# Attention and gated convolution on one core: a new order of all steps, q of batch 0 turned in row pairs, and 46 fillers in four places

## The chip, the cores and the metric

The kernel runs on one core of one Trainium2 chip. The metric is the device time of one execution in microseconds. Work goes to five engines, each with an instruction queue of its own that it works off in order: PE (TensorE, matrix products into the banks of PSUM), DVE (VectorE), ACT (ScalarE), POOL (GpSimd) and SP (SyncE, which only issues transfers here). PE's loading of a stationary operand is listed apart as PEld. Semaphores make an instruction wait for what other engines or transfers must have done.

## The reference

Eight batches, eight heads, 576 tokens, head size 64. First a linear attention without softmax, with a norm over each head, then a gated unit whose gate is a causal convolution over five tokens:

```
kv  = einsum('bhsd,bhse->bhde', k, v)                 # 64 x 64 per batch and head
out = einsum('bhsd,bhde->bhse', q, kv)
x   = out / sqrt(mean(out*out, -1) + 1e-6) * g_norm   # then (B, S, H*D) = (8, 576, 512)
gate_pre[s] = sum over k < 5 of conv_w[k] * x[s - 4 + k]
val = x @ w_val                                       # 512 x 512
result = (sigmoid(gate_pre) * val) @ w_out            # 512 x 512
```

Inputs q, k, v and g_norm are float32; the three weights are stored as float64, so the kernel makes float32 of them itself, in pieces.

## The kernel before

The program is a list of some 1,235 steps, `PLAN`, written out as text; the loop at the end of the kernel calls one small function for each, in that order. The order in the text is the order on each engine's queue; no scheduler changes it. What a step waits for follows from the tiles that it shares with earlier steps. Tiles come from pools with a number of rotating buffers: eight PSUM banks (`ps`), three output tiles `ot`, two `x`, and so on; the next request takes the next buffer in turn.

What the steps do, in the order in which a batch meets them:

- `load_q_rows`, `load_half`, `load_q`, `stage_weight` issue the transfers: q of batches 0 and 1 in two halves by heads, k and v in two halves each, q of later batches by head pairs, the weights in quarters (`wval` 0 to 3, `wout` 0 to 3, and `cw`, the taps of the convolution with g_norm).
- `narrow_weight key n` is one of eight pieces that turn a quarter from float64 into float32: pieces 0, 4, 5, 6 and 7 on DVE, 1, 2 and 3 on ACT. `turn_cw` (PE) and `keep_cw` (DVE) turn the taps.
- `start_warm` runs matmuls of the identity with itself, whose result nobody reads.
- `kv_product b i` (36 matmuls of 64x64, each two rows of the profile) and `kv_copy` (ACT).
- q of batches 0 and 1 is turned on PE by `turn_q_rows` (L477) and put in order by `sort_q` (L484); q of later batches is turned on DVE by `turn_q`.
- `raw_whole` (batch 0, L512), `raw_pair` and `raw_tail` (L501) multiply q by kv; `square`, `sums`, `powers` (POOL, L552) and `normalise` make the norm. Token blocks, called 0 to 3 with 128 tokens and 4 with 64, each have a step.
- `turn_x` (L583) and `keep_x`, or for later batches `turn_blocks` and `move_blocks` (a transfer within SBUF), bring x into columns; `halo` (POOL) copies the rim for the convolution.
- `gate_start`, four `gate_tap` (DVE, L621, 128 of them in all, each adding into the tile that the one before wrote), `gate_end` (the sigmoid, ACT) and `gated` (DVE, L646) make the gate.
- `val_product` (batches 0 and 1, L633) or `val_fast` (L682, seven products in place of eight, with sums of blocks from `x_sums` and `val_sums`) make the values.
- `token_sums` (DVE, L752), `fast_product` (L774), `fast_keep` (DVE or ACT) and `store` make the output of the 512 tokens of a batch pair's halves; `out_product` (L720) that of the last 64 tokens.

At the start of the program the first steps are

```
load_q_rows 0 1; stage_weight cw 0; load_q_rows 0 0; load_half v 0 0; load_half k 0 0; narrow_weight cw 0 5;
...
narrow_weight cw 0 2; warm_up; stage_weight wval 1; stage_weight wval 0; start_warm 36; turn_q_rows 0 3;
turn_q_rows 0 2; turn_q_rows 0 0; kv_product 0 0; turn_q_rows 0 1; sort_q 0 0; sort_q 0 1; narrow_weight cw 0 3;
narrow_weight cw 0 4; narrow_weight cw 0 7; turn_q_rows 0 4; turn_cw; keep_cw; kv_product 0 1; sort_q 0 4;
sort_q 0 3; kv_copy 0 0; kv_copy 0 1; narrow_weight wval 1 5; narrow_weight wval 1 0; sort_q 0 2; raw_whole 0 3;
```

and the functions that the change touches, with what calls them, are:

## Time and profile before

| | |
|---|---|
| time, median of 3 runs | 304.87 us (304.09 to 306.43) |
| span of the profiled execution, first to last instruction | 304.6 us |
| PE busy | 294.8 us, 97% of the span |
| weight loads (PEld) | 232.4 us, 76% |
| DVE busy | 269.2 us, 88% |
| ACT busy | 193.7 us, 64% |
| POOL busy | 114.9 us, 38% |
| moved by transfers | 55.53 MB, 182 GB/s on average |

The profiled execution has no time of its own beside its span. A matmul in float32 stands in the profile as two rows, a transpose as one. Matmuls overlap in PE, so a PE that is always busy may still be slowed: its rate is read from the starts of its rows. The granted clock is 1.00 when PE gets its full rate.

### The profile page before, as it was taken

What the parts mean: (1) busy time and instruction counts of PE and PEld (TensorE: products, weight loads), DVE (VectorE), ACT (ScalarE), POOL (GpSimd) and SP (SyncE); (2) the same over time, 40 slices, a digit from 0 to 9 for tenths busy, and PEclk for the clock granted to TensorE, in tenths of its full rate; (3) what the DMA queues carried; (4) which work ended last, traced back from release to release, by engine and by line L of the source; (5) the groups of instructions that cost most, each with busy time, mean ns of one, the idle gap of its engine ahead of it and who ended that gap; (6) DMA issues with size and microseconds to landing.
All of it is one profiled execution on the core that took longest, in us unless ns stands there. A gap on an engine that the chain in (4) does not pass through costs nothing.

```text
span 304.6 us, 8977 instructions
## 1 busy us (share of the span) xinstructions
PE 294.8 (97%) x3441; PEld 232.4 (76%) x3441; DVE 269.2 (88%) x474; ACT 193.7 (64%) x596; POOL 114.9 (38%) x127
## 2 busy tenths in 40 slices
PE   7899999999999999999999999999999999999993
PEld 7788778877787785777778757787878588888582
DVE  1169999999999999999999999999999999999612
ACT  1569989999768664884586547683787354535220
POOL 3027354406568217364338352345536631000000
PEclk9979999999999999999999999999999999999999
DMA  7999998088569756988689477927411621112423
GB/s 269 343 368 343 272 302 210 4 230 269 154 147 329 231 163 167 269 220 260 173 253 294 111 175 232 326 72 214 114 48 30 169 80 34 36 42 64 103 69 103
DMA packets 32074, 55.53 MB, mean 182 GB/s; under 512 B 6166, under 2 KB 14358, under 8 KB 32032
## 3 DMA queue, kind: packets, MB, share of 16 engines
q1 hardware_dynamic: 29520, 49.76, 55.7%
q0 software_dynamic: 1632, 3.17, 4.1%
q10 hardware_dynamic: 880, 2.03, 1.8%
q8 instruction: 27, 0.44, 0.6%
q14 instruction: 15, 0.12, 0.1%
HBM read 39.21 MB, written 9.44 MB: 160 GB/s over the span
## 4 chain that ended last, share of the span: by engine, by line
PE 89%; DVE 5%; DMA 2%; issue 1%; ACT 1%; DVEq 0%; ACTq 0%; SPq 0%
PE a L774 18%; PE cb L774 14%; PE va L682 13%; PE val L633 11%; PE vc L682 6%; PE kvps L440 6%; PE raw L501 5%; PE out L720 5%; PE vb L682 4%; PE qTps L477 4%; PE raw L512 2%; PE xTps L583 2%; DMA qs<-in_q_dram 2%; DVE gate L621 2%; DVE xs L667 1%
## 5 line engine op out<-in xcount | busy, mean ns | idle before, releaser
L552 POOL TENSOR_TENSOR rt<-ss,mhalf 128x8 f32<-128x8 f32 (+3 forms) x38 | 68.9, 1822 | 101.0 <-DVE ss L544 100.8
L621 DVE SCALAR_TENSOR_TENSOR gate<-xT,cwT,gate 128x576 f32<-128x576 f32 x128 | 101.8, 809 | 1.0
L571 ACT ACTIVATE x<-raw,rt 128x64 f32<-128x64 f32 x252 | 55.8, 351 | 7.2 <-POOL rt L552 4.2
L604 POOL DMA_DIRECT2D xT<-y x48 | 26.4, 557 | 25.5 <-DVE ot L784 14.0
L633 PE MATMUL val<-xT,wval 128*128 128x288 f32 x128 | 33.0, 411 | 0.0
L774 PE MATMUL a<-wsum,sums 128*128 128x256 f32 x128 | 32.4, 382 | 0.0
L628 ACT ACTIVATE gate<-gate 128x576 f32<-128x576 f32 x32 | 22.0, 692 | 11.7 <-DVE gate L621 11.4
L633 PEld LDWEIGHTS val<-xT,wval 128*128 128x128 f32 x128 | 23.5, 190 | 6.5 <-ACT xT L590 0.4
L544 DVE TENSOR_REDUCE ss<-sq 128x8 f32<-128x520 f32 (+1 forms) x40 | 24.7, 627 | 2.9 <-ACT sq L531 2.5
L774 PEld LDWEIGHTS a<-wsum,sums 128*128 128x128 f32 x128 | 24.0, 190 | 4.1 <-issue 0.6
L535 ACT ACTIVATE sq<-raw 128x256 f32<-128x256 f32 (+1 forms) x70 | 22.4, 403 | 7.3 <-PE raw L501 7.1
L682 PE MATMUL va<-xs,vsum 128*128 128x288 f32 x96 | 26.6, 409 | 0.0
L615 ACT ACTIVATE gate<-xT,cwT 128x576 f32<-128x576 f32 x32 | 25.2, 811 | 1.5 <-DVE gv L646 1.3
L646 DVE TENSOR_TENSOR gv<-gv,gate 128x576 f32<-128x576 f32 x32 | 23.6, 750 | 0.9 <-ACT gate L628 0.8
L682 PEld LDWEIGHTS va<-xs,vsum 128*128 128x128 f32 x96 | 18.0, 190 | 5.1 <-ACT x L571 0.4
L611 POOL COPY xT<-xT 128x124 f32<-128x124 f32 x32 | 17.5, 585 | 10.5 <-ACT xT L590 10.5
L501 PEld LDWEIGHTS raw<-kv,qT 64*64 64x64 f32 x1008 | 16.4, 134 | 5.3 <-issue 3.0
L440 PEld LDWEIGHTS kvps<-v,k 64*64 64x64 f32 x1008 | 15.9, 135 | 3.7 <-issue 1.9
L501 PE MATMUL raw<-kv,qT 64*64 64x64 f32 x1008 | 18.7, 221 | 0.0
L440 PE MATMUL kvps<-v,k 64*64 64x64 f32 x1008 | 17.6, 220 | 0.0
L774 PE MATMUL cb<-wsum,sums 128*128 128x256 f32 x64 | 16.9, 386 | 0.1
L774 PE MATMUL cb<-wout,gv 128*128 128x256 f32 x64 | 16.8, 385 | 0.0
(111 smaller groups left out, 542.3 us busy)
## 6 DMA issues: line engine op xcount, KB each, us to landing
qs<-in_q_dram SPq DMA_DIRECT2D x96, 140.0 KB, 4.2
out_dram<-ot SPq DMA_DIRECT2D x140, 64.0 KB, 1.7
k<-in_k_dram SPq DMA_DIRECT2D x14, 576.0 KB, 6.3
v<-in_v_dram SPq DMA_DIRECT2D x12, 576.0 KB, 6.5
xT<-y SPq DMA_DIRECT2D x48, 64.0 KB, 2.7
xT<-y POOLq DMA_DIRECT2D x48, 64.0 KB, 3.3
y<-in_moe_w_val_dram SPq DMA_DIRECT2D x4, 512.0 KB, 11.4
w_wout<-in_moe_w_out_dram SPq DMA_DIRECT2D x4, 512.0 KB, 6.3
```

Source lines behind the costliest of these rows:

```text
L440: nc.tensor.matmul(st["kvps", b][s][r * D:(r + 1) * D, i], st["k", b, i][rows, r, cols], st["v", b, i][rows, r, cols], start=(j == 0), sto ...
L501: nc.tensor.matmul(st["raw", b, c][r][cols, to * D:(to + 1) * D], st["qT", b][rows, hp, first:first + D], kvs[b % 2][rows, hp, :], start=T ...
L544: nc.vector.reduce_sum(out=st["ss", b][:, FIRST[c]:FIRST[c] + n], in_=st["sq", b, c][:, 0:n], axis=AX.X)
L552: nc.gpsimd.tensor_tensor(out=st["rt", b][:, which], in0=st["ss", b][:, which], in1=mhalf[:, which], op=ALU.pow)
L571: nc.scalar.activation(out=x[:, to * D:(to + 1) * D], in_=raw[:, h * D:(h + 1) * D], func=AF.Copy, scale=root[:, to:to + 1])
L604: (nc.sync if i % 2 else nc.gpsimd).dma_start(out=xTs[b % 2][i * TB:(i + 1) * TB, :, first:first + P], in_=y[a * TB:(a + 1) * TB, i])
L615: nc.scalar.activation(out=gate[:], in_=xTs[b % 2][:, jt, HALO:SX], func=AF.Copy, scale=cwT[:, K - 1, jt:jt + 1])
L621: nc.vector.scalar_tensor_tensor(out=gate[:], in0=xTs[b % 2][:, jt, tap * TB:tap * TB + S], scalar=cwT[:, tap, jt:jt + 1], in1=gate[:], op ...
L633: nc.tensor.matmul(val[:], wval[:, kc, jt * P:(jt + 1) * P], xTs[b % 2][:, kc, HALO + n * SV:HALO + (n + 1) * SV], start=(kc == 0), stop=( ...
L646: nc.vector.tensor_tensor(out=both, in0=both, in1=st["gate", b, jt][:], op=ALU.mult)
L682: nc.tensor.matmul(st[bank, "val", b, mj][:], weights_[:, k], tokens()[:, k], start=(n in (0, 1, 3) and k == 0), stop=(k == NK // 2 - 1), ...
L774: nc.tensor.matmul(st[bank, i, p], tokens()[:, k], weights_[:, k], start=(n < 2 and k == 0), stop=(k == NK // 2 - 1), skip_group_check=True)
```

## The change

Every step of `PLAN` stands at a new place, and the pools are gone: each tile that rotated is now one of a fixed set of rooms, and the step's text says which room it takes (`@` and a number; PSUM banks are rooms 0 to 7). q of batch 0 is turned as pairs of rows, 18 transposes of 128x128 in place of 36 matmuls of 64 columns, and sorted by 20 copies of 64 partitions, half on ACT and half on DVE, in place of five on ACT. `kv_copy` of batch 0 is split between ACT and DVE. `start_warm` takes a width: 36 matmuls of 38 columns at the start, and 3, 6 and 1 of 256 columns later, 46 in all. The table of the sigmoid is loaded first.

```diff
+    PAIRED_Q = (0,)
...
+    def new(tag, shape, dtype, name):
+
+        room = rooms[tag][picked.pop(0)]
...
     def ps(shape, name):
-        return psum.tile(shape, FP32, tag="bank", bufs=8, name=name)
+        return new("bank", shape, FP32, name)
...
-    def start_warm(n):
-
+    def start_warm(n, width):
+
+        reps = -(-width // P)
+        bank = ps([TB, reps, width // reps], f"warm{n}")
         for _ in range(n):
-            nc.tensor.matmul(warm_bank()[0:TB, 0, 0:TB], ident[:, 0:TB], ident[:, 0:TB], start=True, stop=True)
+            nc.tensor.matmul(
+                bank[0:TB], ident[:, 0:TB], ident[:, 0:width // reps].unsqueeze(1).broadcast_to((P, reps, width // reps)),
+                start=True, stop=True)
...
             for r in range(2):
                 rows = slice(r * D, (r + 1) * D)
-                nc.scalar.copy(
+                (nc.vector.tensor_copy if r else nc.scalar.copy)(
                     out=kv_bd[rows, :, rows].rearrange("p (i s) e -> p s i e", s=2)[:, s], in_=ps_[rows])
...
+        st["pq", b, j] = pq = ps([P, HB, P], f"qTps{b}_{j}")
+        if b in PAIRED_Q:
+            for r in range(2):
+                for n in range(0, m, 2):
+                    nc.tensor.transpose(
+                        pq[:, r * 2 + n // 2, :],
+                        qs[:, r, j * HB + n:j * HB + n + 2, :].rearrange("p n d -> p (n d)"), ident[:])
+            return
...
+        for r in range(2):
+            for e in range(2):
+                (nc.vector.tensor_copy if b == 0 and r else nc.scalar.copy)(
+                    out=qT[r * D:(r + 1) * D, j * HB + e:j * HB + m:2],
+                    in_=pq[e * D:(e + 1) * D, r * 2:r * 2 + m // 2])
```

The new list begins and ends with

```
load_q_rows 0 1; load_q_rows 0 0; load_half v 0 1 @ 0; load_half k 0 1 @ 0; start_warm 36 38 @ 0;
load_half v 0 0 @ 0; stage_weight wval 1; warm_up; load_half k 0 0 @ 0; stage_weight wval 0;
stage_weight cw 0 @ 0; turn_q_rows 0 4 @ 1; turn_q_rows 0 2 @ 0; turn_q_rows 0 1 @ 2; turn_q_rows 0 3 @ 3;
sort_q 0 1 @ 0; turn_q_rows 0 0 @ 4; start_warm 3 256 @ 5; sort_q 0 0; load_q_rows 1 0; stage_weight wval 3;
sort_q 0 3; load_q_rows 1 1; sort_q 0 2; kv_product 0 1 @ 2 4; stage_weight wval 2; load_half k 1 1;
narrow_weight cw 0 0 @ 0; start_warm 6 256 @ 3; narrow_weight cw 0 5 @ 0; load_half v 1 1;
narrow_weight cw 0 1; sort_q 0 4; narrow_weight cw 0 2; narrow_weight cw 0 3; narrow_weight wval 1 0 @ 1;
stage_weight wout 0 @ 1; narrow_weight cw 0 4; narrow_weight wval 1 1; narrow_weight cw 0 6 @ 1;
narrow_weight cw 0 7; narrow_weight wval 1 2; turn_cw @ 1; kv_product 0 0; keep_cw; load_half v 1 0;
narrow_weight wval 1 5 @ 1; narrow_weight wval 1 3; narrow_weight wval 1 6 @ 0; start_warm 1 256 @ 1;
kv_copy 0 1; kv_copy 0 0; load_half k 1 0; narrow_weight wval 0 0 @ 0; raw_whole 0 4 @ 3;
...
gate_end 7 2; gated 7 3; fast_product 3 1 6; gated 7 2; fast_product 3 1 5; fast_keep 3 1 6;
token_sums 3 1 0 @ 1; store 3 3; out_product 3 8 @ 2; fast_keep 3 1 5; token_sums 3 1 2 @ 2; token_sums 3 1 1;
store 3 2; token_sums 3 1 3; fast_product 3 2 1 @ 0; fast_product 3 2 3; fast_keep 3 2 1 @ 0; keep_out 3 8 @ 1;
...
```

In the instruction order of the two kernels the numbers differ only in what is named here: PE has 18 transposes more, 36 matmuls of q less and 10 wide fillers more; DVE has 12 copies more; ACT has two copies more and one table load less; SP and POOL have as many instructions as before. Of DVE's 128 taps, 27 stood directly behind a tap of the same gate, and 10 do now; of the sums of blocks (`x_sums`, `token_sums`) 10 stood directly behind the one that they read, and 3 do now.

## The prediction

> **What bounds the kernel now.** I read the engines' totals first, then busy time by stretch with the granted clock, then the matrix engine's timeline, then VectorE's timeline; last, the waits and the instruction order of the two kernels. The totals:

> ```profile
> PE 294.8 (97%) x3441; PEld 232.4 (76%) x3441; DVE 269.2 (88%) x474; ACT 193.7 (64%) x596; POOL 114.9 (38%) x127
> ```

> Two engines are near full. By stretch (columns: length, then busy us of PE, weight loads, DVE, ACT, POOL, then granted clock, DMA share, GB/s):

> ```profile
> 13.90:17.10 3.20, 1.53 (x73) 1.39 (x73) 2.29 (x8) 1.67 (x6) 0.00 (x0) 1.00 0.75 239
> 17.10:17.70 0.60, 0.55 (x2) 0.35 (x2) 0.60 (x3) 0.55 (x3) 0.00 (x0) 0.70 1.08 438
> 17.70:21.10 3.40, 3.40 (x20) 2.84 (x20) 1.80 (x4) 2.99 (x5) 0.17 (x1) 0.55 1.01 371
> ...
> 15.84:32.00 16.16, 15.60 (x254) 13.68 (x246) 13.37 (x26) 13.77 (x27) 8.75 (x5) 0.89 0.96 347
> 32.00:200.00 168.00, 167.36 (x2233) 129.31 (x2232) 166.54 (x284) 124.04 (x407) 75.81 (x83) 1.00 0.76 218
> 200.00:283.77 83.77, 83.52 (x646) 66.43 (x645) 81.00 (x132) 46.96 (x145) 27.95 (x32) 1.00 0.30 80
> ```

> Between 32 and 200 us both PE and VectorE run at 99%: there is nearly nothing idle to win there. What is lost lies in the first 30 us: PE works 1.53 of 3.20 us at 13.9 to 17.1, and the clock granted just after is 0.55. PE's timeline shows it:

> ```profile
> 1.36 4.05 PE L430 MATMUL warm<-ident 128*32 128x32 f32 x72 [1.36 <-POOL ident masks.py:199]
> 6.12 5.05 PE L477 MATMUL qTps<-ident,qs 128*64 128x128 f32 x48 [0.70 <-DMA qs<-in_q_dram]
> 15.05 0.21 PE L414 MATMUL cwps<-ident,cw 21*128 21x21 f32 x1 [1.22 <-issue]
> 17.15 6.32 PE L512 MATMUL raw<-kvbd,qT 128*128 128x128 f32 x40 [0.56 <-ACT kvbd L450]
> 23.40 2.84 PE L477 MATMUL qTps<-ident,qs 128*64 128x128 f32 x48
> 30.23 1.09 PE L583 MATMUL xTps<-ident,x 128*128 128x128 f32 x8
> ```

> The same 48 rows of q take 5.05 us at the start and 2.84 later: the start runs cold, though no throttle record marks it. The 40 rows of raw (128 columns each, 0.11 us warm as in xTps, half of that for the eight 64-wide ones, 3.8 to 4.0 in all) take 6.3: 2.3 us are lost to the clock.

> **PE's work from raw on.** At full rate, by the rows of the chain of waits (two fast products in 1.73 us, a fast val piece 0.97, four plain val products 7.96, a tail product 3.58): 112 fast products x 0.863 = 96.7; 84 val pieces x 0.97 = 81.5; 16 val products x 1.94 = 31.0; 4 tails 14.0; 14 kv products x 1.05 = 14.7; raw 15.5 + 4.0; q and x turns 9.4. That is 266.8. Each passage between wide matmuls and the 64x64 ones costs about 0.1 us; these edges sum to 9.3, so 276.1. Measured from 17.15 to the end of the last matmul at 299.3: 282.2. The rest, 6.1, is 2.3 of clock and 3.8 of true waits: 0.8 for the last token sums at 288.0, 0.4 before 282.5, some 0.4 before 31, 2.2 spread.

> **The change, part by part.**
> Row pairs: q of batch 0 takes 18 transposes instead of 36 matmuls. A 128-column transpose is 0.11 us warm (the eight rows of xTps from 30.23 to the first val at 31.16), so 2.0 us instead of 4.2; cold, twice that. In exchange sort_q grows from five copies to twenty of 64 partitions, ten on ACT (0.35 us by qT 128x256) and ten on DVE (0.42 by the copy at L797), DVE's each behind ACT's for the same part. DVE adds 4 us, before its dense stretch begins, where it idled 5.2 and 6.7 us.

> The walk to raw: q lands at 6.12 as before (the two q loads still lead their queues). With the clock full from 7.4 the ten transposes that sort_q 0 1 needs end near 8.0, all 18 at 8.7; three fillers (0.43 each) follow. ACT's four sorts end at 11.0, DVE's at 11.9. The pieces of cw are queued behind them: DVE's first at 12.0, ACT's three (0.40 each, with the last sort between) until 13.8, DVE's last three (0.28) until 14.8. turn_cw follows at 14.85 (15.05 before). kv product and copies: 15.0 to 16.2, then DVE's copy, queued behind keep_cw and two pieces of wval (1.6 us), ends at 17.2. Splitting kv_copy over two engines saves 0.5 and gives it back there. So raw starts at 17.25, against 17.15: I expect no gain. If all q work were warm from 6.1 and DVE did not queue, 16.1; if the clock stayed half until 14.2, 20.0. I take 17.25, since only the fillers' width (38 for 32, which closes 5.4 to 5.9) changes ahead of it.

> The ten fillers of 256: 4.3 us of PE, hidden in PE's idle time before cw and kv data. If that cover is gone (cold, twice the price) they push turn_cw itself. They fill the gap that preceded the half clock: 14.2 to 17.7 goes from 1.9 to about 2.2 busy us of 3.4, and the stretch before it from 3.0 to 3.2. Whether that suffices no row shows; the nearest kept stretch, 10.8 to 13.9, was 98% busy. Bounds: raw in 4.0 or 6.3. I take 4.0: gain 2.3.

> [...]

> After raw: turn_q_rows 1 0 is given the bank that normalise 0 3 still reads (0.2 us late by POOL's 2.06 us power), the turns of x wait for ACT 0.65 in all. Waits before the first val product 0.85 instead of 0.4.

> New order, DVE: an operation that uses the result just ahead of it starts later:

> ```profile
> 267.83 3.25 DVE L621 SCALAR_TENSOR_TENSOR gate<-xT,cwT,gate 128x576 f32<-128x576 f32 x4
> ...
> 169.22 0.79 DVE L621 SCALAR_TENSOR_TENSOR gate<-xT,cwT,gate 128x576 f32<-128x576 f32 x1
> 169.94 0.44 DVE L689 TENSOR_TENSOR gv<-vc,gv 128x288 f32<-128x288 f32 x1
> ```

> Four taps of one gate take 0.81 us each; a tap with a stranger behind it gives way after 0.72. In the order, taps directly behind a tap of the same gate fall from 27 to 10, dependent sums from 10 to 3: 24 x 0.1 = 2.4 us off DVE. That is no gain by itself: PE is as full. It is bounded by 0 and 2.9.

> DVE's own end: from the first piece of wval to the last gated 260.9 us busy (the three DVE numbers above), plus 2.0 for cw, keep_cw and kv copies now behind it, less 2.4, started at 13.6, with the 4.2 idle of before after 32 and 0.4 early: 278.7; with the 20.0 from there to the end, 298.7. So PE sets the end.

> New order, PE: 24 groups of 64x64 matmuls instead of 26 and 31 wide stretches instead of 35: edges 8.5, not 9.3. At the end the first token sum no longer stands behind a keep that waits for PE, and out_product 3 8 (3.6 us) covers it: the 0.8 at 288.0 goes, and I drop the 0.4 ahead of it. The other 2.2 I leave; 0 and 5 are its bounds. SP's loads of batch 1's q go out near 9 instead of 14 and 17, and DMA idle at 14 to 16 (152 GB/s) is used; nobody waits for it.

> **Sum.** 17.25 + 275.3 + 0.85 + 2.2 = 295.6 for the last matmul; 5.3 behind it as now (299.3 to 304.6): a span of 300.9. The page gives the profiled execution its span alone, 304.6; the median of the runs, 304.87, lies 0.27 above. So 301.2.

> **Rivals.**
> The fillers don't hold the clock: raw at half rate, 301.2 + 2.3 = 303.5. For it: 2.2 of 3.4 us is still far from the kept 98%. Against: no gap is as long as 1.2.

> Cold start, the other side. Transposes and 32-column fillers may not warm the clock: the 72 warm rows did not in 4 us, and no row here shows a transpose doing so. Then 18 transposes take 3.9, three fillers 2.6, kv 2.4, six fillers up to 5.2, in PE's order ahead of turn_cw. If the first full clock comes at 17.7, raw starts at 21.2 and the end is 305.2; with raw at half clock as well, 307.5. It is slower than before from a raw start near 21 on. Against it: the q matmuls alone warmed it by 10.8. [...]

> New waits in the middle: with PE and DVE both at 99%, one wrong order makes each wait for the other. 3 us more gives 304.2, 7 gives 308.2. For it: 32 to 200 was nearly free of waits, so there is more to lose than to win; rooms are now fixed by hand. Against: DVE gets 2.4 us of air.

> Better: the 2.2 of waits vanish and raw starts at 16.1: 297.9.

> **How the numbers follow.** Forecast 0.45 (own range 299.5 to 302.8), better 0.16, fillers fail 0.13, middle waits 0.16, cold start 0.10. A measurement here tells about 1% from nothing, so faster means below 301.8: seven tenths of the forecast, 0.32, all of better, and a little of the others make 0.50. Slower, above 307.9, is the far part of middle waits and of the cold start: 0.12. The rest, 0.38, is same. The range reaches from better to the cold start: 297.8 to 305.4.

> **What would show it.** Raw (40 rows) starting at 17 to 17.5 and taking 4 us at clock 1.00; cwps near 14.9; 18 transposes in 2 to 3 us from 6.1; the first val near 28.4; DVE busy for 2 us less at the same work; no wait of cb for sums near the end. I am wrong if the clock falls before 21 us, if raw starts after 20, or if PE's waits between 32 and 284 exceed 5 us.

## The result, and the profile after

The changed kernel takes 307.13 us (median of 8 runs, 305.69 to 308.16), the kernel before 304.75 (8 runs, 304.09 to 306.43). The ratio is 1.007, 95% interval 1.0044 to 1.0096: slower by 0.7%, where the prediction said 301.2 and at most 305.4.

One number first, since the sum rests on it. In every execution whose time and span are both known, the time is the span plus 1.74 to 1.90 us. After's profiled execution has a span of 306.4 and took 308.16, the slowest of its eight. Before's, with a span of 304.6, was therefore the run of 306.43, the slowest of its three, and not one near the median. Of 88 later executions of before, 57 have a mean granted clock of 0.995 or more and a median of 304.29 us, 31 a lower one (mostly 0.993) and a median of 306.05. The execution that the prediction was read from has 0.993.

After's totals, then busy time by stretch (length, PE, weight loads, DVE, ACT, POOL, granted clock, DMA share, GB/s):

```profile
PE 294.8 (96%) x3407; PEld 231.4 (76%) x3407; DVE 272.5 (89%) x486; ACT 194.1 (63%) x598; POOL 111.5 (36%) x127
```

```profile
13.90:17.10 3.20, 1.84 (x48) 1.08 (x47) 2.67 (x11) 2.60 (x5) 0.00 (x0) 1.00 1.06 375
17.10:17.70 0.60, 0.60 (x33) 0.54 (x33) 0.35 (x1) 0.00 (x0) 0.00 (x0) 1.00 1.15 395
17.70:21.10 3.40, 3.06 (x31) 2.40 (x27) 2.89 (x7) 2.38 (x6) 0.00 (x0) 1.00 1.07 379
15.84:32.00 16.16, 15.24 (x277) 13.05 (x274) 15.23 (x33) 12.71 (x24) 8.85 (x7) 1.00 1.05 387
32.00:200.00 168.00, 166.21 (x2237) 130.68 (x2236) 164.85 (x284) 122.80 (x400) 76.11 (x80) 1.00 0.73 205
200.00:285.64 85.64, 84.16 (x647) 66.32 (x646) 80.24 (x130) 48.50 (x152) 24.15 (x32) 1.00 0.36 92
```

The clock is 1.00 in every stretch, as the fillers were expected to make it. But between 32 and 200 us PE is busy for 166.2 us where it was for 167.4, and DVE for 164.9 where it was for 166.5: both wait more. PE's timeline of the head:

```profile
6.28 2.66 PE L513 MATMUL bank<-ident,qs 128*128 128x128 f32 x18
11.97 2.78 PE L463 MATMUL bank<-ident 128*32 128x256 f32 x12
15.52 0.21 PE L450 MATMUL bank<-ident,cw 21*128 21x21 f32 x1 [0.78 <-ACT wexp L404]
15.66 0.81 PE L475 MATMUL bank<-v,k 64*64 64x64 f32 x39
17.05 0.73 PE L475 MATMUL bank<-v,k 64*64 64x64 f32 x33 [0.58 <-issue]
18.66 4.43 PE L560 MATMUL bank<-kvbd,qT 128*64 128x128 f32 x40 [0.34 <-DVE kvbd L485]
29.86 2.21 PE L681 MATMUL bank<-xT,wval 128*128 128x288 f32 x8
```

The 18 transposes take 2.7 us and the 40 rows of raw 4.43, but raw starts at 18.66 instead of 17.25: the turn of cw is late, the kv product stops after 39 rows for 0.58 us with nothing to wait for, and the first product with wval comes at 29.86, not 28.4. In the middle, these lines of the list of waits (waiter, releaser: total us, times, longest) matter:

```profile
ACT ot L835 <- DMA out_dram<-ot: 5.8, 5, 1.9
ACT ot L833 <- DMA out_dram<-ot: 4.8, 4, 3.4
PE bank L821 <- ACT ot L833: 1.4, 4, 0.4
PE bank L631 <- ACT gv L690: 0.8, 1, 0.8
```

ScalarE's copies of the fast products (L833, L835) wait 10.6 us for stores to leave an output tile; before had 5.7 of such waits, 4.2 of them in one where nothing was behind it. The timeline of one case (chosen rows):

```profile
221.30 8.99 SPq L853 DMA_DIRECT2D out_dram<-ot  x11
224.48 1.13 PE L730 MATMUL bank<-xT,wval 128*128 128x288 f32 x4
225.59 0.37 ACT L833 COPY ot<-bank 128x256 f32<-128x256 f32 x1 [3.37 <-DMA out_dram<-ot]
226.02 1.13 PE L821 MATMUL bank<-wsum,w 128*128 128x256 f32 x4 [0.40 <-ACT ot L833]
228.30 0.44 ACT L837 COPY ot<-bank 128x256 f32<-128x256 f32 x1
228.79 1.13 PE L821 MATMUL bank<-wsum,w 128*128 128x256 f32 x4 [0.68 <-ACT ot L837]
```

ScalarE stands still for 3.4 us, until the tile's store has landed. SP issues the store in pieces, one behind the other. The row of SP above merges two groups with a pause between them: eight pieces from 221.30 to 226.1, the next ones from 229.0. The fourth piece is issued at 222.81 and lands 2.68 us later, at 225.49, and the copy starts at 225.59. PE needs the copied bank and waits; so does the next copy. I count PE's waits as what each step lasts beyond the same step in an undisturbed place: behind 31 us they sum to 7.2 us in after and 3.5 in before. The chain that ended last says it in shares of the span:

```profile
PE 63%; DVE 11%; DMA 9%; ACT 7%; SPq 5%; issue 3%; POOL 1%; ACTq 0%; DVEq 0%; POOLq 0%
```

It was 89% PE before.

### The profile page after: what moved, and what is told of

Same layout as the page of the kernel before. It is cut to its first block, busy times and chain, and to the rows that moved or that the text cites. A ratio compares the mean times of both kernels' runs of the same rounds, so it can differ in the third digit from the quotient of the medians.

```text
span 306.4 us, 8926 instructions
## 1 busy us (share of the span) xinstructions
PE 294.8 (96%) x3407; PEld 231.4 (76%) x3407; DVE 272.5 (89%) x486; ACT 194.1 (63%) x598; POOL 111.5 (36%) x127
## 4 chain that ended last, share of the span: by engine, by line
PE 63%; DVE 11%; DMA 9%; ACT 7%; SPq 5%; issue 3%; POOL 1%; ACTq 0%; DVEq 0%; POOLq 0%
PE bank L821 24%; PE bank L730 16%; PE bank L681 7%; DMA out_dram<-ot 6%; PE bank L549 5%; PE bank L475 5%; PE bank L768 5%; SPq L853 4%; DVE gate L669 3%; DMA qs<-in_q_dram 2%; ACT x L619 2%; ACT gate L676 1%; DVE qT L532 1%; DVE ss L592 1%; PE bank L631 1%
## 5 line engine op out<-in xcount | busy, mean ns | idle before, releaser
L619 ACT ACTIVATE x<-bank,rt 128x64 f32<-128x64 f32 x252 | 55.8, 376 | 3.8 <-POOL rt L600 3.5
L821 PE MATMUL bank<-wsum,w 128*128 128x256 f32 x192 | 49.2, 386 | 2.1 <-ACT ot L833 1.4
L821 PEld LDWEIGHTS bank<-wsum,w 128*128 128x128 f32 x192 | 35.3, 190 | 10.1 <-ACT ot L833 3.2
L730 PE MATMUL bank<-xs,vsum 128*128 128x288 f32 x144 | 38.7, 408 | 0.0
L681 PE MATMUL bank<-xT,wval 128*128 128x288 f32 x128 | 33.1, 411 | 0.0
L821 PE MATMUL bank<-wout,gv 128*128 128x256 f32 x128 | 32.6, 383 | 0.1
L730 PEld LDWEIGHTS bank<-xs,vsum 128*128 128x128 f32 x144 | 27.1, 190 | 7.4 <-issue 0.4
L681 PEld LDWEIGHTS bank<-xT,wval 128*128 128x128 f32 x128 | 23.6, 190 | 6.1
L821 PEld LDWEIGHTS bank<-wout,gv 128*128 128x128 f32 x128 | 23.9, 190 | 4.3 <-ACT ot L835 0.5
L730 PE MATMUL bank<-xT,wval 128*128 128x288 f32 x96 | 26.2, 408 | 0.2 <-issue 0.2
L583 ACT ACTIVATE sq<-bank 128x256 f32<-128x256 f32 (+1 forms) x70 | 21.3, 382 | 7.1 <-PE bank L549 7.0
L730 PEld LDWEIGHTS bank<-xT,wval 128*128 128x128 f32 x96 | 17.9, 190 | 5.0 <-issue 0.3
L475 PEld LDWEIGHTS bank<-v,k 64*64 64x64 f32 x1008 | 16.4, 135 | 4.9 <-issue 2.8
```

The costliest lines, as they stand in the source:

```text
L475: nc.tensor.matmul(st["kvps", b][s][r * D:(r + 1) * D, i], st["k", b, i][rows, r, cols], st["v", b, i][rows, r, cols], start=(j == 0), sto ...
L619: nc.scalar.activation(out=x[:, to * D:(to + 1) * D], in_=raw[:, h * D:(h + 1) * D], func=AF.Copy, scale=root[:, to:to + 1])
L681: nc.tensor.matmul(val[:], wval[:, kc, jt * P:(jt + 1) * P], xTs[b % 2][:, kc, HALO + n * SV:HALO + (n + 1) * SV], start=(kc == 0), stop=( ...
L730: nc.tensor.matmul(st[bank, "val", b, mj][:], weights_[:, k], tokens()[:, k], start=(n in (0, 1, 3) and k == 0), stop=(k == NK // 2 - 1), ...
L821: nc.tensor.matmul(st[bank, i, p], tokens()[:, k], weights_[:, k], start=(n < 2 and k == 0), stop=(k == NK // 2 - 1), skip_group_check=True)
```

## The experiments

The runs stood in four groups on four chips, each with before beside it, whose median lay between 304.34 and 305.12 us. A difference between runs of two groups is therefore read from their ratios to before as well as from their medians.

The theory after this reading: the head loses against before, and three output tiles with the new order of stores make ScalarE wait, then PE. The rival: the new order interlocks PE and VectorE whatever the rooms.

### Five output tiles instead of three

The two tiles of `wexp` are free once the weights are narrowed; each row takes the tile that is free longest.

```diff
+    rooms["ot"] = rooms["ot"] + rooms["wexp"]
-fast_keep 0 0 1 @ 0; ... fast_keep 0 0 0 @ 1; ... fast_keep 0 1 0 @ 2
+fast_keep 0 0 1 @ 3; ... fast_keep 0 0 0 @ 4; ... fast_keep 0 1 0 @ 2
```

> The kernel after, with five rooms for rows of the output instead of three (the two rooms of wexp are free once the weights are narrowed; each row takes the room that has been free the longest). Nothing else is moved. Theory 1 (the late loss is ScalarE's copies waiting for stores to free a room: 10.6 us of such waits after, of which some 3 us of the matrix engine's 7.2 us of waits behind 31 us): the waits of ScalarE's copies for stores fall under 2 us, the matrix engine's waits at 196 to 227 us go, and the time falls by 1.5 to 3 us, to 304 to 305.6. Theory 2 (the new order interlocks the matrix engine and VectorE whatever the rooms): ScalarE waits less, but the end moves by less than 0.7 us.

Measured: 303.77 us (12 runs), ratio to before 0.9959 (0.9936 to 0.9981), 3.4 us less than after. One wait of these copies for a store is left, near the end:

```profile
ACT ot L830 <- DMA out_dram<-ot: 2.2, 1, 2.2
```

PE's waits behind 31 us fall from 7.2 to 3.1, and the chain is back at 85% PE. The first theory holds, at slightly more than its upper bound.

The steps of this run are those of after, rooms included, up to the first copy of a fast product. Its head should thus be after's, but its profile, of an execution of 302.96 us, is ahead of it:

```profile
14.86 0.20 PE L447 MATMUL bank<-ident,cw 21*128 21x21 f32 x1 [0.78 <-ACT wexp L401]
17.43 4.43 PE L557 MATMUL bank<-kvbd,qT 128*64 128x128 f32 x40 [0.34 <-DVE kvbd L482]
28.63 2.21 PE L678 MATMUL bank<-xT,wval 128*128 128x288 f32 x8
```

So 1.2 us of what after's profile lost in the head belong to that execution, the slowest of its eight, and not to the order; the prediction's 14.85, 17.25 and 28.4 fit this execution within 0.25 us.

The control was before's whole order with five tiles:

> Before's whole order in the code of after, with five rooms for rows of the output instead of three. Theory 1 (it is after's order that is short of rooms; before's waits for stores are 1.5 us, and 4.2 at the end where nothing is behind them): 303.8 to 304.6, no change. Theory 2 (three rooms are too few for any order): 302.5 or less.

Measured: 304.06 (12 runs; before beside it 305.12, with a mean clock below 0.995 in 8 of 23 executions; ratio 0.9969, 0.9941 to 0.9997; the same order with three tiles gave 304.26 on another chip). PE's waits are 3.9 with three tiles and 3.9 with five. So it is after's order that is short of tiles; a small gain for before's order is not excluded by that ratio.

### Before's order in after's code

```diff
-    PAIRED_Q = (0,)
+    PAIRED_Q = ()
```

with before's list of steps, rooms taken in turn, and kv copied by ScalarE alone.

> The code of after with the whole order of the kernel before: q of batch 0 not in pairs, kv copied by ScalarE alone, 36 fillers of 32 columns and no wide ones, rooms taken in turn. Nothing but the explicit rooms differs from the kernel before. Theory 1 (explicit rooms cost nothing of themselves): 304.2 to 305.2, and granted clocks of 0.993 and 0.997 both occur, as they do in the 25 runs of before (medians of the two kinds 305.3 and 304.2). Theory 2 (explicit rooms make instructions wait where the pools did not): 306 to 307.5, which would also explain why after's head with before's order came to 307.05.

Measured: 304.26 (12 runs), ratio 1.0002 (0.9983 to 1.0021). Rooms cost nothing. Its profile is of an execution with the clock up, and gives the baseline that the prediction lacked:

```profile
5.97 3.04 PE L515 MATMUL bank<-ident,qs 128*64 128x128 f32 x48 [0.56 <-DMA qs<-in_q_dram]
13.62 0.23 PE L446 MATMUL bank<-ident,cw 21*128 21x21 f32 x1 [1.46 <-DVE cw L421]
15.70 4.96 PE L556 MATMUL bank<-kvbd,qT 128*128 128x128 f32 x40 [0.56 <-ACT kvbd L481]
28.57 2.11 PE L677 MATMUL bank<-xT,wval 128*128 128x288 f32 x8
```

The same order that reached the turn of cw at 15.05, raw at 17.15 and the first product with wval at 31.16 does so here at 13.62, 15.70 and 28.57. In the profiled execution of before the first 48 rows of q had taken 5.05 us, here 3.04; raw had taken 6.32, here 4.96. That execution was thus late by 1.4 us up to raw and by 2.6 at the first product. Against this, after's head is later by 1.3 us at the first product with wval in after's profile and by 0.1 in that with five tiles; at equal work by 1.0 us more, since eight rows of turned x were already done here. The chain of this profile is 68% PE, at a lower time than the one with 89%: the share of the chain alone says little.

### The fillers alone, in before's order

```diff
-start_warm 36 32
+start_warm 36 38
 turn_q_rows 0 4;
+start_warm 3 256;
 turn_cw; keep_cw; kv_product 0 1;
+start_warm 1 256;
```

> The run above, and the first 36 fillers 38 columns wide, three fillers of 256 columns ahead of the turn of cw and one ahead of raw: the fillers alone. Theory A (the clock of raw is worth what the runs of before show, 1.1 us in half of them): every run has a clock of 0.996 or more, and the median lies 0.4 to 0.7 us below that of the run above. Theory B (2.3 us, as raw's duration in the one profile of before says): 2 us below.

Measured: 304.38 (11 runs), ratio 0.9991 (0.9975 to 1.0007). All 11 lie between 304.17 and 304.70 with a clock of 0.995 or more; without fillers the same order had 12 runs between 303.96 and 306.14. The fillers hold the clock in all 11, where 31 of 88 executions of before lose it, and the runs above 305 are gone. The median does not move, because the usual run of before has no loss for them to save: less than either theory.

### After without the wide fillers, with three tiles and with five

```diff
-start_warm 3 256; ... start_warm 6 256; ... start_warm 1 256;
```

> The kernel after, without its ten fillers of 256 columns; the 36 of 38 columns stay. Theory A (the fillers hold the clock): the granted clock halves again between 13 and 19 us, raw's 40 rows take about 6.3 us instead of 4.4, and the time rises by 1.5 to 2.5 us, to about 309. [...]

Measured with three: 307.43 (12 runs), 0.3 more than after. The clock does halve, raw takes 6.7, and the first product with wval comes 1.7 us later. A stretch (columns as above), and two pieces of PE's timeline:

```profile
13.90:17.10 3.20, 2.31 (x73) 2.18 (x73) 2.33 (x9) 2.16 (x3) 0.00 (x0) 0.50 1.07 378
```

```profile
14.79 0.26 PE L446 MATMUL bank<-ident,cw 21*128 21x21 f32 x1 [3.47 <-ACT wexp L400]
18.09 6.71 PE L556 MATMUL bank<-kvbd,qT 128*64 128x128 f32 x40 [0.92 <-DVE kvbd L481]
```

Theory A was right about the clock and wrong about the end: by the two profiles (after's is that of its slowest run) 1.4 of the 1.7 us was swallowed behind, PE's waits falling from 7.2 to 3.9. That fits a middle that runs against its stores. So the same with five tiles:

> Five rooms for rows of the output, and without the ten wide fillers. Without them but with three rooms the first product with wval started 1.7 us later (31.57 for 29.86) and the end moved by 0.3 only. Theory 1 (with three rooms the waits for stores swallowed the 1.4): with five rooms the whole loss reaches the end, 303.77 + 1.7 = 305.5, from 304.9 to 306. Theory 2 (the matrix engine's start is not what the end hangs on, VectorE is): 303.8 to 304.4.

Measured: 306.2 (7 runs), 2.4 more than with fillers, 4.0 by the ratios (1.009 and 0.9959), and above the first theory's range. With tiles enough, the head's time reaches the end. The 1.7 us expected was too small: it was read against after's slow execution. Against the profile with five tiles and fillers (28.63) the first product with wval comes 3.9 us later, at 32.52.

### Two halves joined

After's steps up to the first gate, then what is left in before's order:

```diff
 keep_x 0 1; narrow_weight wval 2 7;
-gate_start 0 0; narrow_weight wout 0 0; gate_start 0 3; ...
+sort_q 1 0; sort_q 1 3; load_half k 2 0; kv_product 1 0; ... gate_start 0 0; ...
```

> The code of after, with after's order up to the two loads of x columns ahead of the first gate, and from there on the steps that are left in the order of the kernel before; rooms taken in turn. Theory 1 (the head wins 1.3 us and the order behind it loses more): 304.75 - 1.3 = about 303.4, from 302.5 to 304.3, and the matrix engine's waits behind 31 us stay near before's 3.5 us. Theory 2 (the head's lead is lost whatever order comes behind it, because VectorE or the loads set the pace): 304.5 to 305.5.

Measured: 307.05 (8 runs), ratio 1.0084 (1.0049 to 1.0119). Both theories took after's head to be 1.3 us ahead; against before's usual run it is behind, and PE's waits behind 31 us are 4.6. Then the reverse, before's steps up to the first product with wval and after's rest:

> The code of after, q of batch 0 not in pairs, no wide fillers, before's order up to the first product with wval, and from there on the steps that are left in after's order; rooms taken in turn, ready-made. Theory 1 (after's order behind the head costs 3.7 us of waits more than before's): 304.75 + 3.7 = about 308.4, from 307.3 to 309.5. Theory 2 (after's order behind the head is no worse; its waits come from what the new head brings forward): 304.3 to 305.5.

Measured: 312.57 (6 runs). Of 12.5 us of waits 3.6 stand in one place at the seam (inside the pair of raw 1 3, for ScalarE's copy of kv, until 43.6) and 1.3 ahead of the turn of x at 52.9. After's rest counts on steps that its own head has done, so this run tells the theories apart no further.

### Three local moves

With five tiles, three waits of PE were left that a change of place should remove: at 46.7 in after's profile, for one, the turn of x waits for a copy that stands on ScalarE behind a normalisation, which itself waits 1.97 us for POOL's power:

```profile
45.94 0.93 ACT L619 ACTIVATE x<-bank,rt 128x64 f32<-128x64 f32 x4 [1.97 <-POOL rt L600]
46.73 0.72 ACT L690 COPY gv<-bank 128x288 f32<-128x288 f32 x2
47.50 0.44 PE L631 MATMUL bank<-ident,x 128*128 128x128 f32 x2 [0.80 <-ACT gv L690]
```

```diff
-normalise 1 4; sums 1 3; raw_pair 1 1; keep_val 0 2 1; gate_tap 0 1 0; keep_val 0 1 0;
+sums 1 3; raw_pair 1 1; keep_val 0 2 1; gate_tap 0 1 0; keep_val 0 1 0; normalise 1 4;
-normalise 6 3; sums 6 0; ... fast_keep 2 1 0;
+fast_keep 2 1 0; normalise 6 3; sums 6 0; ...
-fast_product 3 2 5; fast_keep 3 2 0; store 3 8; fast_product 3 2 2;
+fast_keep 3 2 0; ... fast_product 3 2 2; fast_product 3 2 5; store 3 8;
```

> Five rooms, and three local moves: the normalisation 1 4 behind the copy of val 0 1 0 on ScalarE (wait of 0.87 us at 44.3), the copy of fast product 2 1 0 ahead of the normalisation 6 3 (0.49 at 199.4), and the copy of fast product 3 2 0 and the product 3 2 2 ahead of the product 3 2 5 (0.62 at 285.4). Theory 1 (each of the matrix engine's waits is paid in full, since nothing else is late): the three waits fall from 1.98 to 0.5 us together, and the time to 302.3, from 301.9 to 302.9. Theory 2 (VectorE or ScalarE is late next, and the waits turn up elsewhere): 303.3 to 304.1.

Measured: 301.72 (6 runs), ratio 0.9911 (0.9890 to 0.9931): 2.05 us less than with five tiles alone, 1.5 by the ratios. The three waits are gone from the list. The first theory holds, a little below its range; together 5.4 us of after's time (4.8 by the ratios) lay in a short stock of tiles and three places in the order.

### The head: pairs, cw, loads, program

With the middle open, what the head costs can be read at the end. First the pairs:

```diff
-    PAIRED_Q = (0,)
+    PAIRED_Q = ()
-start_warm 3 256; ... start_warm 6 256;
+start_warm 1 256; ... start_warm 3 256;
```

> The run with five rooms and three moves, but q of batch 0 not in pairs: 36 matmuls and five copies of ScalarE in place of 18 transposes and twenty copies by ScalarE and VectorE; four wide fillers ahead of the turn of cw instead of nine, since the matrix engine is busy for 2.1 us more there. Theory 1 (the pairs cost: the twenty copies stand ahead of the pieces of cw, whose turn starts at 14.9 with pairs and at 13.6 in before's order): the turn of cw starts near 13.8, raw near 16.8 instead of 18.0, and the time falls from 301.72 by 0.7 to 1.3, to 300.4 to 301.0. Theory 2 (the pairs win their 2.1 us of matmuls): the turn of cw at 16 or later and 302.5 to 304. Theory 3 (hidden both ways): within 0.5 of 301.72.

Measured: 301.56 (6 runs), ratio 0.9883 (0.9855 to 0.9910); within 0.2 us of the run with pairs by the medians, which is theory 3. By the ratios it is 0.9 us less, which is theory 1; the two runs stood on different chips and their intervals overlap, so these are not told apart. Theory 2 is out. Raw starts 0.9 earlier, at 17.15, less because of cw (its turn is at 14.57) than because the kv product no longer stops. Instead PE stops later:

```profile
67.89 2.34 PE L679 MATMUL bank<-xT,wval 128*128 128x288 f32 x9 [1.04 <-issue]
```

Then the turn of cw out of the way:

```diff
-turn_cw; kv_product 0 0; keep_cw; ... raw_whole 0 4;
+kv_product 0 0; ... raw_whole 0 4; turn_cw; keep_cw;
```

> The run with five rooms and three moves, with the turn of cw and its copies moved from ahead of the second kv product of batch 0 to behind raw's first four rows. Theory 1 (raw starts late because the turn of cw holds the matrix engine's order up): the kv product starts at about 14.2 instead of 15.0, raw at about 17.1 instead of 18.0, and the time falls by 0.5 to 0.9, to 300.8 to 301.2. Theory 2 (the load of k sets the kv product anyway, or VectorE's copies set raw): raw starts at 17.8 or later and the time stays within 0.4 of 301.72.

Measured: 303.06 (12 runs), 1.3 more, 0.7 by the ratios (0.9933 here): neither theory. The kv product does start at 14.14, and then stops for 1.62 us. PE's timeline, and one transfer queue between 14 and 15 us (packets, MB, share):

```profile
14.14 0.85 PE L474 MATMUL bank<-v,k 64*64 64x64 f32 x41
16.61 0.69 PE L474 MATMUL bank<-v,k 64*64 64x64 f32 x31 [1.62 <-issue]
```

```profile
q8 instruction: 1, 0.02, 7.1%
```

That packet is 16,384 bytes of program, moved from 14.1 to 15.2. In the four runs with this stop (after, after's head with before's rest, the three moves, and this one) PE goes on 1.2 to 1.4 us after the packet's end, at whatever time that is. Moving the product forward only moved it into the gap. In the run with five tiles alone, with after's steps, the packet was through at 14.44 instead of 15.82, and the same product lasted 1.56 us where it takes 1.28 undisturbed, with one short stop until 15.82, which is again 1.4 us after the packet. To shift the ends of the pieces, 54 fillers of 25 columns instead of 36 of 38, and in the unpaired order 14 of 97:

```diff
-start_warm 36 38
+start_warm 54 25
```

> The run with five rooms and three moves, with 54 fillers of 25 columns in place of 36 of 38: about the same time on the matrix engine, 36 more rows in its program. In that run, in after and in two others the second kv product of batch 0 stops after 39 to 41 rows for 0.5 to 1.6 us for nothing but issue, and goes on 1.2 to 1.4 us after a 16 KB transfer of program ends. Theory 1 (the matrix engine has run through its piece of program, and 36 rows more put the end of the piece elsewhere): the stop at 16.4 is gone, raw starts at 17.5 instead of 18.0, and the time falls from 301.72 by 0.4 to 0.6. Theory 2 (the stop comes from the busy transfers of data): it stays.

> The unpaired run, with 14 first fillers of 97 columns in place of 36 of 38. With 44 rows less ahead the matrix engine's pieces of program would end where they do in the run with pairs, which stops for nothing but issue only at 16.4. Theory 1 (the stops of 1.0 us at 66.9 and 0.4 at 145.5 in the unpaired run are ends of pieces): they go, one of about 0.5 may come back in the second kv product, and the time falls from 301.56 to 300.3 to 301. Theory 2 (they are waits of the order): the time stays within 0.4.

Measured: 301.44 (6 runs), ratio 0.9882 (0.9848 to 0.9916), and 301.46 (6 runs), ratio 0.9870 (0.9837 to 0.9903). In both profiles the stop is gone, with 54 fillers

```profile
15.20 1.28 PE L473 MATMUL bank<-v,k 64*64 64x64 f32 x72
```

and in the unpaired order those at 66.9 and 146.6 too; PE's waits behind 31 us are 1.1 and 1.0, among the least of all. Rows ahead thus move the stops, which fits the theory of pieces; how long a stop lasts goes with when its packet comes, and what sets that no run shows. In time the gain is 0.3 and 0.1 us by the medians, less than the 0.4 and 0.6 expected at the least, and below what these runs resolve.

Last, the order of the loads:

```diff
-load_half v 0 0; stage_weight wval 1; warm_up; load_half k 0 0;
+load_half v 0 0; load_half k 0 0; stage_weight wval 1; warm_up;
```

with two pieces of wval 1 (0 on VectorE, 1 on ScalarE) behind cw's pieces; the expectation names only the first.

> The unpaired run, with the load of k's first half ahead of the load of the second column block of wval, as before's order has it, and the first piece of that block behind the pieces of cw. What is open: raw starts at 18.7 in after and 17.15 in the unpaired run, but at 15.7 with before's order. Theory 1 (the loads' order: 512 KB of wval at about 0.38 MB per us stand ahead of k, and VectorE waits for them in front of cw's last pieces): the turn of cw at 14.0, the kv product at 14.2, raw at 16.2 to 16.4, and the time falls from 301.56 by 0.5 to 0.9. Theory 2 (wval then is late and the first product with it waits): raw early, but the first product with wval no earlier than 28.3, and the time within 0.4 or up.

> The two runs above together: unpaired, k early, 14 first fillers of 97 columns. If both gains stand on their own: 301.56 - 0.8 - 0.7 = about 300.1, from 299.5 to 300.8; if either is eaten by VectorE (full from 17 us on), 300.8 to 301.6.

Measured: 302.6 (7 runs) and 303.03 (10 runs), 1.0 and 1.6 more than without. The kv product comes at 14.71, but ScalarE's copy of it, at 17.62, now stands behind three pieces of wval that come later, and VectorE's copy, at 17.90, waits for ScalarE's:

```profile
14.71 1.28 PE L473 MATMUL bank<-v,k 64*64 64x64 f32 x72
18.45 4.43 PE L558 MATMUL bank<-kvbd,qT 128*64 128x128 f32 x40 [1.92 <-DVE kvbd L483]
```

and the first product with wval is at 29.65. The time is theory 2's, but raw is late too, which neither theory had. In the second run the clock takes part: five executions with a mean clock of 0.991 to 0.994 took 303.16 to 303.72 us, the five others 301.75 to 302.90. Why raw starts at 15.7 with before's order and no earlier than 17.15 with any head of after's is not settled by one cause: the loads' order is part of it, but can't be changed without that of VectorE's and ScalarE's pieces.

## Why the prediction was wrong, by its own steps

**The baseline.** "The page gives the profiled execution its span alone, 304.6; the median of the runs, 304.87, lies 0.27 above" is the first step that failed. The time is 1.8 us above the span, which alone moves the sum from 301.2 to 302.7. And the profiled execution had lost time that the median run does not lose: "17.25, against 17.15: I expect no gain" compares with a raw that starts at 15.70 in an execution with the clock up.

**The clock term** ("I take 4.0: gain 2.3") followed from that. The mechanism was right: clock 1.00 throughout, raw in 4.43 (0.111 a row, the narrow ones no cheaper). Its worth in before's median run is nothing, as the fillers alone showed. In after's own head, with five tiles, the fillers are worth 2.4 us. The sign "the clock falls before 21 us" did not come to pass.

**Raw at 17.25** came at 18.66 in the profiled execution and at 17.43 in that with five tiles, from the same steps; as a reading of the order the step was right. In after's profile VectorE's sorts ended at 12.4 (11.9 was said; 11.7 with five tiles) and cw's turn came at 15.52 (14.85), a delay of 0.67; the stop in the kv product cost 0.58, and nothing in the prediction looked for one. Behind the stop ScalarE's kv copy waits 0.83 us for the product, and VectorE's 0.66 for ScalarE's.

**PE's work.** 275.3 was said. From 18.66 to the last matmul's end at 301.8 (counted as the prediction does) are 283.1 us; less 7.6 of waits leaves 275.5. The work and its edges were right.

**The waits** are the term that made most of the difference, and it was mis-sized: "The other 2.2 I leave; 0 and 5 are its bounds" and 0.85 ahead of the first product, against 7.6 in all. The rival "new waits in the middle" had this, with "rooms are now fixed by hand" for it, at 0.16. What it missed was to follow the output tiles: who frees them (SP's store pieces, one behind the other at some 0.4 us each, in one queue with loads that themselves wait), and who is queued behind the copy that waits. Its counter-argument, 2.4 us of air for VectorE, is an engine's total; VectorE did come out lighter (268.0 us without the 4.5 of new copies, 269.2 before), which is 1.2 us and not 2.4, but a mean does not keep a queue from standing still. Of the prediction's own signs of being wrong one came: PE's waits between 32 and 284 are some 6.6 us, and 5 was its limit. That these waits came from the stock of tiles is shown by the two tiles more: 3.1 us of waits and 3.4 us less time.

**The end.** The "0.8 for the last token sums at 288.0" was no wait of PE. Only a weight load waited there, while PE still ran the tail product: from that product's start to the next step are 3.59 us, as at 118.4 in the same profile, and 3.58 in after. There was nothing to drop. A new wait of 0.6 us came behind the product at 290.7. From the last matmul to the end are 4.6 us, not 5.3.

**The sum again:** 295.6 + 1.4 (raw) + 4.6 (waits) + 0.2 = 301.8; + 4.6 = 306.4, the span; + 1.8 = 308.2, which is the profiled run of after, the slowest of its eight.

**Gaps and the clock.** The prediction argued from the length of gaps ("no gap is as long as 1.2"). In the traces the length alone does not decide. Both profiles without wide fillers have a gap of 3.47 us, and all 19 runs of these two have a mean clock of 0.979 to 0.989; but the clock fell 1.4 us into that gap with three tiles (at 12.75) and 2.2 us into it with five (at 14.08). Gaps of 1.46 and 0.56 did not halve it in the profile of before's order, and 1.2 and 0.6 did in the first one.

| profile | stretch of 3.41 us, from | PE busy in it | clock after it |
|---|---|---|---|
| before, the first profile | 13.93 | 1.73 | halved |
| no wide fillers, three tiles | 9.33 | 1.57 | halved |
| no wide fillers, five tiles | 10.67 | 1.25 | halved |
| before's head, after's rest | 40.43 | 0.22 | halved |
| before's head, after's rest | 13.12 | 1.85 | kept |
| no wide fillers, five tiles | 7.25 | 1.87 | kept |
| before's order | 12.80 | 2.01 | kept |
| after | 14.12 | 2.05 | kept |

While the clock is full, at most 1.73 us busy in a stretch and it falls, at least 1.85 and it stays, in all 17 profiles up to the last matmuls. At the very end, where only wide products run, 1.42 and 1.47 us were still enough in two profiles, so the bound is not busy time alone. The grid does not lie at the same place in every execution: with the same steps up to there, it has a line at 5.92 us in one profile without wide fillers and the next ones at 9.33 and 12.75, in the other at 7.25, 10.67 and 14.08. So gaps of the same length can fall into one stretch or be parted by its edge, which fits that before has the lower clock in 31 of 88 executions; what sets the place of the grid no run shows. The fillers' mechanism in the prediction, to fill the stretch ahead of raw, was right: 1.73 us of it were busy before, 2.05 after.

## What to carry to other kernels

Before a sum is made against a profiled execution, find out which of the timed runs it is: the span and the clock of each run tell, and a loss that only one profile shows is not there to be won in the median. When an order is replanned around fixed buffers, follow each buffer to the engine that frees it last, here an output tile to the queue of its store, and price what stands behind the instruction that waits for it. The best version here (five output tiles, three moves, first fillers that move PE's stops, with q of batch 0 in pairs or not) takes 301.4 to 301.5 us, 1.2 to 1.3% less than before; the worth of that move is not resolved in it. Of the 5.7 us that it is faster than after, 3.4 came with two tiles that stood unused once the weights were narrowed.

## What the runs showed of the hardware

The program comes in packets of 16,384 bytes (queue 8, instruction: 27 of them in before's profile, 27 in after's), and beside such packets the matrix engine can stop for nothing but issue: up to 1.6 us in the kv product, 1.0 at 66.9 among products with wval, going on 1.2 to 1.5 us after the packet's end. That each packet is a piece of PE's program, and that the rows run through a piece faster than the next one comes, is my reading; it fits these stops, and that they were gone with 54 and with 14 first fillers, and no run shows it by itself.

The 18 transposes of 128 columns ran in 2.2 to 2.8 us straight behind narrow fillers, and the clock record of after stands at 1.00 from 7.29 to 304.25: they did not make the start cold, which was one of the rivals. Nor did they let the clock fall: without wide fillers and with three tiles, PE's 2.29 busy us of the stretch from 5.92 to 9.33 are nearly all transposes, and the clock stayed at 1.00 until 12.75.
